# Products k'v by head in half-column tiles, one state update per pair of batches, and new hand-written orders, in a gated linear attention kernel with a GELU MLP

## The chip, the cores and the metric

The kernel runs on one core of one Trainium2 chip. The core has a matrix engine (TensorE, PE in the profile, with PEld for its weight loads), a vector engine (VectorE, DVE), an activation engine (ScalarE, ACT), GpSimd (POOL) and a synchronising engine (SyncE, SP); the last two mostly issue transfers here. Each engine takes its instructions in the order in which the program gives them; semaphores make one engine wait for another. The metric is the time of one execution on the device in microseconds, lower is better.

## The reference

Per batch and head, a state of 48x48 decays row by row with a gate and takes up an outer product at each of 768 steps; the output of a step is the query times the state. The results of the 8 heads side by side (384 values a token) go through a two-layer MLP with the tanh form of GELU.

```python
batch, n_heads, seq, head_dim = (4, 8, 768, 48)
for t in range(S):
    state = alpha[:, :, t, :, None] * state + np.einsum('bhd,bhe->bhde', k[:, :, t], v[:, :, t])
    y[:, :, t] = np.einsum('bhd,bhde->bhe', q[:, :, t], state)
...
n_tokens, d_model, d_ff = (3072, 384, 2048)
h = x @ w_in
g = 0.5 * h * (1.0 + np.tanh(c * (h + 0.044715 * h * h * h)))
return (g @ w_out).astype(np.float32)
```

## The kernel before

**Tiling.** The 768 steps are cut into 6 chunks of 128. Batches go two at a time, so there are 12 "pairs" m = 0 to 11: pair m is chunk m // 2 of batches 0 and 1 (m even) or 2 and 3 (m odd). Inside a chunk the recurrence becomes products. With b the running product of the gates, q' = q b (`qp`) and k' = k / b (`kp`), the output is mask(q' k'^T) v plus q' times the state that the chunk starts with, and the next state is (k'^T v + state) times the last row of b.

**A pair, step by step**, by the names that its tasks carry: `ln` (ACT, logarithm of the gate), `cum` (PE, running sums by a triangular matrix), `b` and `binv` (ACT, exponentials), `qp` and `kp` (DVE), `t` and `ev` (transposes of q' and k' on PE and their copies out; in pairs 6 to 11 the transfer `turn` instead), `attn` (PE, line 552: k' times q' per head, and in pairs 2 to 11 also line 561: q' times the old state), `mask` (DVE, line 571), `y` (PE, lines 617 and 627), `x` (copy out), `tx` and `xe` (transposing x; a `turn` in pairs 6 to 11), `kv` (PE, line 581) and `st` (DVE, lines 606 and 608). Then the MLP of that pair: eight tasks `l1` (PE, line 658, six products of 256 columns each), eight `gelu` (ACT), `l2` (PE, line 677, four products of 384 columns a task, four tasks a batch), `ot` (copy out on ACT or DVE) and `store` (SP).

**Heads in 64 places.** q' and k' hold each head in 64 columns, 48 filled and 16 zero, so that two heads fill the 128 columns of the array, and after the transposes two heads lie on top of each other in rows 0 to 63 and 64 to 127. Lines 484, 552 and 561 use the array cut into two halves by rows, one head in each (in the profile 64\*128).

**kv and st before.** Line 581 takes a pair of heads at once: 128 weight columns (both k' heads) times 96 columns of v (both v heads). Of the four 48x48 blocks of the result two are of use, head with head; the other two, head with the other head, are carried along unused. A batch has four such products, and the state of a batch is a tile of 128 x (4 x 96). `carry` then adds the old state (line 606, DVE; not in chunk 0) and multiplies by the last row of b (line 608, DVE), one task for each batch. `attn` reads the useful block of the state: `st[sl, p, self.D * o:self.D * o + self.D]`. Pairs 0 and 1 are laid out differently ("packed"): their k' is turned back (line 516) before kv, batch by batch.

**What sets the order.** A planner class holds tasks with costs (`W`, `COST`), and `FIRST` gives a list of steps such as `P:kv2.0` (PE, task kv of pair 2, first one) that fixes the order of all tasks on all engines. The list is complete, so each engine's order is that list. `fill` steps are idle products on zeros in the early part of PE's order. The planner's costs decide nothing where the list is complete. A list `firsts` made every `l2` task depend on all first-layer tasks of pairs 0 and 1. PSUM is shared out in tagged buffers; kv, y and the transposes share the tag `yk` with two buffers.

Of the kernel before, what the change touches and what calls it, by code (L numbers as in the profile page):

```python
# [17 lines left out]
    qk2=910, qk1=500, ev8=650, ev4=350, mask=640, st=1090, st0=545, tr=270, attn2=590, inter2=220, vb=320, vb_act=480, ring=1300, ring_issue=670, out=2050, lead=600, receipt=1400, receipt_hw=1000, xc=520, xe=330, ot=540,  # L18
# [153 lines left out]
class _Kernel:  # L172
# [21 lines left out]
        P:tx1.1 V:xe1.1 A:gelu0.5 P:l10.6 P:l11.0 A:gelu0.6 P:l11.4 P:l11.3 P:l11.5 A:gelu1.0 A:gelu1.4 A:gelu1.3 P:l11.2 A:gelu1.5 A:gelu1.2 P:l11.7
        A:gelu1.7 P:l11.1 P:l11.6 A:gelu1.1 P:l20.0 A:ln2.0 P:l20.3 P:l20.7 P:cum2.0 P:kv1.0 P:l20.11 P:l20.4 A:b2.0 A:binv2.0 A:ln2.1 P:cum2.1 A:b2.1
        V:st1.0 V:kp2.0 V:qp2.0 P:kv1.1 V:st1.1 G:load.33 G:load.34 G:load.35 G:load.36 G:load.37 V:qp2.1 P:l20.1 G:load.38 P:l20.5 P:l20.8 A:binv2.1
        V:kp2.1 A:gelu1.6 V:tr2.0 V:tr2.1 P:t2.0 A:ev2.1 V:ev2.0 V:tr2.2 V:tr2.3 P:l20.12 G:load.39 G:load.40 G:load.41 G:gate.2 G:load.42 G:gate.3
        G:load.43 G:gate.4 G:load.44 A:ot0.0 P:l20.15 P:attn2.0 A:ot0.3 P:l20.2 V:mask2.2 V:mask2.3 P:l20.9 P:l20.6 A:ln3.0 P:cum3.0 A:b3.0 V:mask2.0
        V:mask2.1 P:y2.0 P:l20.13 V:x2.0 P:y2.1 A:x2.1 V:qp3.0 P:l20.10 P:tx2.0 A:binv3.0 P:tx2.1 A:ot0.1 V:xe2.0 V:xe2.1 P:l20.14 A:ot0.2 P:kv2.0
        V:kp3.0 P:l12.6 P:l12.0 A:gelu2.0 A:gelu2.6 P:l12.5 V:st2.0 P:t3.0 A:gelu2.5 P:l12.1 A:ev3.1 V:tr3.0 P:l12.3 V:tr3.1 V:ev3.0 P:kv3.0 P:l12.7  # L200
        P:kv2.1 A:gelu2.1 P:l12.4 A:gelu2.7 A:gelu2.3 A:gelu2.4 P:l12.2 V:tr3.2 P:l22.4 V:tr3.3 V:st3.0 V:st2.1 P:attn3.0 A:gelu2.2 P:l22.5 P:l22.6
        V:mask3.2 V:mask3.3 A:ln4.0 P:cum4.0 P:l22.0 A:ln5.0 V:mask3.0 V:mask3.1 A:b4.0 P:y3.0 P:l22.7 A:x3.0 P:y3.1 P:kv3.1 V:qp4.0 P:l22.1 A:binv4.0
        A:x3.1 P:l22.2 A:ot2.1 P:tx3.1 V:st3.1 S:store0.0 V:tr4.0 V:xe3.1 P:cum5.0 P:tx3.0 V:xe3.0 V:kp4.0 P:l22.3 P:l13.0 A:binv5.0 A:b5.0 A:ot2.0
        P:l13.3 S:store0.3 P:t4.0 V:tr4.1 V:tr4.2 V:tr4.3 S:store2.1 V:ev4.0 P:l13.4 P:l13.2 V:ev4.1 P:kv4.0 A:gelu3.0 A:gelu3.3 A:gelu3.2 A:gelu3.4
        P:l13.5 A:gelu3.5 G:gate.5 G:load.45 G:gate.6 G:load.46 G:gate.7 G:load.47 G:gate.8 G:load.48 G:gate.9 G:load.49 G:gate.10 G:load.50 G:gate.11
        G:load.51 G:gate.12 G:load.52 G:gate.13 G:load.53 G:gate.14 G:load.54 G:gate.15 G:load.55 G:gate.16 G:load.56 G:gate.17 G:load.57 G:gate.18
        P:kv4.1 P:l13.6 P:l13.1 A:gelu3.6 P:l13.7 V:st4.0 V:st4.1 P:attn4.0 A:gelu3.1 P:l23.0 P:l23.1 A:gelu3.7 S:store2.0 S:store0.1 V:qp5.0 V:tr5.0
        A:ln6.0 V:mask4.2 V:mask4.0 V:mask4.3 V:mask4.1 V:kp5.0 P:l23.2 P:y4.0 P:l23.3 V:ot3.0 S:store3.0 P:y4.1 A:x4.0 A:x4.1 P:cum6.0 P:l23.4 A:b6.0
        P:tx4.0 V:xe4.0 P:tx4.1 V:xe4.1 P:l23.5 A:binv6.0 V:qp6.0 P:t5.0 A:ev5.1 A:ln7.0 V:ev5.0 P:l23.6 P:l23.7 P:attn5.0 P:l14.0 A:ot3.1 V:tr6.0
        V:tr5.1 V:tr5.2 V:mask5.0 S:store0.2 P:l14.4 P:l14.3 V:mask5.1 A:gelu4.0 A:gelu4.4 S:turn6.0 P:l14.6 S:store3.1 A:gelu4.3 A:gelu4.6 V:mask5.2  # L210
        V:mask5.3 P:y5.0 A:x5.0 V:kp6.0 V:tr6.1 V:tr6.2 P:l14.5 V:tr5.3 P:l14.2 A:gelu4.5 A:gelu4.2 P:y5.1 P:l14.1 A:gelu4.1 P:l14.7 P:kv5.1 V:x5.1
        V:tr6.3 P:kv5.0 A:gelu4.7 P:l24.0 P:cum7.0 A:b7.0 A:binv7.0 V:st5.1 P:l24.4 V:st5.0 P:kv6.0 S:turn6.1 V:st6.0 V:qp7.0 P:l24.5 P:l24.1 P:l24.2
        A:ln8.0 P:tx5.0 P:tx5.1 P:cum8.0 V:xe5.1 V:xe5.0 V:kp7.0 A:binv8.0 P:l24.3 V:ot4.0 P:l24.6 A:b8.0 P:l24.7 A:ot4.1 P:attn6.0 V:mask6.0 P:l15.0
        V:mask6.1 P:l15.2 P:l15.4 P:l15.5 V:mask6.2 V:kp8.0 V:mask6.3 P:y6.0 A:gelu5.0 A:gelu5.2 A:gelu5.4 P:l15.6 P:l15.1 V:x6.0 A:gelu5.6 A:gelu5.5
        P:y6.1 V:qp8.0 A:x6.1 S:turn7.0 P:l15.3 P:kv6.1 P:l15.7 A:gelu5.1 P:l25.4 S:turn7.1 P:l25.0 A:gelu5.3 P:l25.5 P:l25.6 A:gelu5.7 A:ln9.0
        V:st6.1 P:attn7.0 P:l25.1 V:mask7.2 P:l25.7 V:mask7.3 G:load.58 G:gate.19 G:load.59 G:gate.20 G:load.60 S:turn6.2 P:l25.2 A:ot5.1 V:mask7.0
        P:cum9.0 A:binv9.0 G:gate.21 G:load.61 G:gate.22 V:mask7.1 V:tr8.0 P:l25.3 P:y7.0 P:y7.1 P:l16.0 V:ot5.0 V:tr7.0 V:tr7.1 A:gelu6.0 A:x7.0
        P:l16.5 P:l16.7 P:l16.3 V:x7.1 S:store4.0 S:turn8.0 P:kv8.1 P:kv8.0 A:gelu6.7 A:gelu6.5 A:gelu6.3 S:turn7.2 V:tr8.1 V:tr8.2 P:l16.6 A:gelu6.6
        P:l16.4 A:gelu6.4 P:l16.1 P:l16.2 A:gelu6.1 A:gelu6.2 V:tr8.3 V:st8.1 V:st8.0 V:tr7.2 V:tr7.3 P:kv7.1 V:st7.1 V:kp9.0 P:kv7.0 P:l26.0 P:l26.1
        P:l26.4 P:l26.5 P:l26.2 S:turn8.1 A:ln10.0 A:b9.0 V:tr9.0 V:tr9.1 V:tr9.2 V:tr9.3 G:load.62 G:gate.23 G:load.63 G:gate.24 G:load.64 G:gate.25  # L220
        V:qp9.0 P:cum10.0 A:binv10.0 P:l26.3 P:l17.0 P:l26.6 P:l26.7 A:ot6.0 A:b10.0 S:turn9.1 A:gelu7.0 P:l17.6 A:gelu7.6 V:ot6.1 V:st7.0 P:l17.1
        A:gelu7.1 P:l17.2 P:l17.3 A:gelu7.2 P:attn8.0 S:turn9.0 V:mask8.0 V:mask8.1 A:gelu7.3 P:l17.7 P:l17.4 A:gelu7.4 A:gelu7.7 P:l17.5 V:mask8.2
        A:gelu7.5 P:l27.0 G:load.65 P:y8.0 V:mask8.3 A:x8.0 P:l27.4 P:y8.1 P:l27.5 P:l27.6 P:l27.1 V:x8.1 V:qp10.0 P:kv9.0 V:kp10.0 A:ln11.0 P:cum11.0
        A:binv11.0 A:b11.0 P:l27.7 P:l27.2 S:turn8.2 P:l27.3 S:store4.1 V:st9.0 P:attn9.0 V:kp11.0 S:store5.1 V:qp11.0 A:ot7.0 A:ot7.1 S:turn10.1
        P:l18.0 S:turn10.0 A:gelu8.0 S:store6.1 P:l18.3 V:mask9.0 V:mask9.1 P:l18.1 A:gelu8.1 A:gelu8.3 P:l18.7 P:l18.5 V:mask9.2 S:turn11.1 V:mask9.3
# [479 lines left out]
    def tasks(self):  # L705
# [221 lines left out]
        n = 0  # L927
# [108 lines left out]
```

## Time and profile before

| | |
|---|---|
| median of 3 runs | 174.98 us (174.98, 182.13, 174.59) |
| the profiled execution, its own time | 173.77 us |
| its span, first to last instruction | 171.9 us |
| clock granted to TensorE | 1.000 |
| DMA traffic | 29.40 MB, mean 171 GB/s |
| transfers out to landing, stores of 192 KB | 3.0 us |

The profile is one execution. It gives the busy time of each engine, the busy share in 40 slices, the chain of work that ended last, the groups of instructions by source line with their mean durations and the idle time ahead of them, and the transfers. The time of a product in these views is its latency, not its share of the stream; what it costs the stream is read from the starts of neighbours.

### The profile page before, as it was taken

What the parts mean: (1) busy time and instruction counts of PE and PEld (TensorE: products, weight loads), DVE (VectorE), ACT (ScalarE), POOL (GpSimd) and SP (SyncE); (2) the same over time, 40 slices, a digit from 0 to 9 for tenths busy, and PEclk for the clock granted to TensorE, in tenths of its full rate; (3) what the DMA queues carried; (4) which work ended last, traced back from release to release, by engine and by line L of the source; (5) the groups of instructions that cost most, each with busy time, mean ns of one, the idle gap of its engine ahead of it and who ended that gap; (6) DMA issues with size and microseconds to landing.
All of it is one profiled execution on the core that took longest, in us unless ns stands there. A gap on an engine that the chain in (4) does not pass through costs nothing.

```text
span 171.9 us, 4595 instructions
## 1 busy us (share of the span) xinstructions
PE 166.3 (97%) x1909; PEld 129.8 (75%) x1909; DVE 107.7 (63%) x210; ACT 125.5 (73%) x205; POOL 63.0 (37%) x88
## 2 busy tenths in 40 slices
PE   7999999999999999999999999999999999999991
PEld 2566899666886896797697797796797978987860
DVE  6499820588978999998892898865947550100100
ACT  4578889897999798899779499868882636651412
POOL 2396546986504674933565435320000000000000
PEclk9999999999999999999999999999999999999999
DMA  4999999999999999999999999897967504001212
GB/s 138 311 268 217 199 247 230 231 230 228 256 208 96 257 218 241 169 165 242 145 224 213 158 226 138 181 233 60 232 186 148 147 1 114 4 0 40 101 48 92
DMA packets 51541, 29.40 MB, mean 171 GB/s; under 512 B 39616, under 2 KB 47936, under 8 KB 51520
## 3 DMA queue, kind: packets, MB, share of 16 engines
q0 software_dynamic: 26464, 17.70, 62.3%
q1 hardware_dynamic: 24512, 11.01, 30.8%
q10 hardware_dynamic: 544, 0.39, 0.8%
q8 instruction: 15, 0.25, 0.6%
q14 instruction: 6, 0.05, 0.1%
HBM read 25.17 MB, written 4.72 MB: 174 GB/s over the span
## 4 chain that ended last, share of the span: by engine, by line
PE 91%; DMA 3%; ACT 3%; DVE 0%; issue 0%; DVEq 0%
PE hT L658 37%; PE acc L677 37%; PE at L552 4%; DMA k<-in_k_dram 3%; PE yps L627 2%; PE cum L416 2%; PE kv L581 2%; PE qkT_ps L484 1%; PE xT_ps L646 1%; PE qkT_ps L470 1%; PE yps L561 1%; ACT qkT L508 1%; PE k_ps L516 1%; ACT L318 1%; PE idle L327 1%; PE yps L617 1%
## 5 line engine op out<-in xcount | busy, mean ns | idle before, releaser
L658 PE MATMUL hT<-xT,w_in 128*128 128x256 bf16 x576 | 69.4, 273 | 0.0
L677 PE MATMUL acc<-w_out,gT 128*128 128x384 bf16 (+3 forms) x416 | 68.9, 314 | 0.0
L664 ACT ACTIVATE gT<-hT 128x512 bf16<-128x512 f32 x96 | 53.6, 600 | 15.2 <-PE hT L658 13.1
L658 PEld LDWEIGHTS <-w_in 128*128 128x128 bf16 x576 | 60.6, 114 | 1.2 <-DMA w_in<-in_moe_w_in_dram 0.3
L677 PEld LDWEIGHTS <-gT 128*128 128x128 bf16 x416 | 37.4, 98 | 20.2
L571 DVE TENSOR_TENSOR atm<-at,ut 128x512 bf16<-128x512 f32 x48 | 30.1, 683 | 8.2 <-PE at L552 8.0
L689 DVE COPY ot<-acc 128x384 f32<-128x384 f32 (+2 forms) x9 | 4.3, 488 | 20.0 <-PE acc L677 20.0
L689 ACT COPY ot<-acc 128x384 f32<-128x384 f32 (+1 forms) x17 | 7.9, 472 | 11.6 <-PE acc L677 9.3
L595 DVE STREAM_TRANSPOSE tr<-b 32x256 f32<-32x256 f32 x32 | 14.0, 438 | 1.4 <-ACT b L449 0.8
L346 POOL DMA_DIRECT2D k<-in_k_dram x11 | 12.2, 1111 | 5.7 <-DMA v<-in_v_dram 1.7
L346 POOL DMA_DIRECT2D a<-in_alpha_dram x11 | 12.3, 1117 | 4.4 <-issue 1.7
L460 DVE TENSOR_TENSOR qp<-q,b 128x768 bf16<-128x768 f32 (+1 forms) x15 | 11.9, 792 | 2.8 <-ACT b L449 2.6
L346 POOL DMA_DIRECT2D vb<-in_v_dram x11 | 12.2, 1105 | 3.6 <-issue 1.9
L346 POOL DMA_DIRECT2D q<-in_q_dram x11 | 12.2, 1112 | 2.5 <-DMA w_out<-in_moe_w_out_dram 1.0
L449 ACT ACTIVATE binv<-cum 128x768 bf16<-128x768 f32 (+1 forms) x15 | 10.1, 684 | 3.3 <-PE cum L416 3.3
L460 DVE TENSOR_TENSOR kp<-k,binv 128x768 bf16<-128x768 f32 (+1 forms) x15 | 11.9, 791 | 0.5 <-ACT binv L449 0.5
L318 ACT ACT_TABLE_LOAD x9 | 11.5, 1283 | 0.9 <-PEq L1020 0.7
L449 ACT ACTIVATE b<-cum 128x768 f32<-128x768 f32 (+1 forms) x15 | 10.3, 685 | 2.0 <-PE cum L416 1.5
L664 ACT ACT_TABLE_LOAD x9 | 11.5, 1283 | 0.2
L606 DVE TENSOR_TENSOR stmp<-kv,st 128x384 f32<-128x384 f32 x16 | 8.9, 555 | 1.9 <-PE kv L581 1.2
L608 DVE TENSOR_TENSOR st<-stmp,tr 128x384 bf16<-128x384 f32 x16 | 8.9, 558 | 0.6
L399 ACT ACTIVATE la<-a 128x768 f16<-128x768 f32 (+1 forms) x11 | 8.5, 784 | 0.1
(74 smaller groups left out, 144.8 us busy)
## 6 DMA issues: line engine op xcount, KB each, us to landing
out_dram<-ot SPq DMA_DIRECT2D x19, 192.0 KB, 3.0
a<-in_alpha_dram POOLq DMA_DIRECT2D x9, 384.0 KB, 7.8
q<-in_q_dram POOLq DMA_DIRECT2D x9, 384.0 KB, 8.8
k<-in_k_dram POOLq DMA_DIRECT2D x9, 384.0 KB, 6.9
vb<-in_v_dram POOLq DMA_DIRECT2D x9, 192.0 KB, 6.3
w_in<-in_moe_w_in_dram POOLq DMA_DIRECT2D x4, 384.0 KB, 8.9
w_out<-in_moe_w_out_dram POOLq DMA_DIRECT2D x4, 384.0 KB, 11.0
out_dram<-ot SPq DMA_DIRECT2D x9, 96.0 KB, 1.9
```

The costliest lines, as they stand in the source:

```text
L318: nc.scalar.add_instruction(mybir.InstLoadActFuncSet(name=nc.get_next_instruction_name(), act_func_set_id=i, engine=mybir.EngineType.Activ ...
L346: dma(u[t][:, lo:hi].rearrange("t b h d -> t (b h) d"), src.rearrange("b h s d -> s (b h) d")[c * C:(c + 1) * C])
L449: self.nc.scalar.activation(u[n].rearrange("t i h d -> t i (h d)")[:, lo:hi], cum, AF.Exp, scale=1.0 if n == "b" else -1.0)
L460: self.nc.vector.tensor_tensor(out, rows, b, op=ALU.mult)
L571: self.nc.vector.tensor_tensor(u["atm", i][:, o], u["at", i][o], self.ut[:, None, :].to_broadcast([self.C, self.H // 2, self.C]), op=ALU.mult)
L595: self.nc.vector.transpose(u["tr"][f:f + 32, :, 0:32], rows[:, lo:lo + H * 2 * D].rearrange("t (g n) -> t g n", n=2 * D)[:, :, 0:32])
L606: nc.vector.tensor_tensor(s, acc, old, op=ALU.add)
L608: nc.vector.tensor_tensor(new, acc, end[:, :, None].to_broadcast([C, H // 2, 2 * D]), op=ALU.mult)
L658: self.nc.tensor.matmul(h[:, s].rearrange("p (g t) -> p g t", t=self.C), w_in[:, j, nt % 4 + s], self.xT[c % self.NX][:, lo:hi, j], start= ...
L664: return lambda e: self.nc.scalar.activation(self.gT[c % self.NG][:, nt:nt + 2, lo * self.C:hi * self.C], f.pop(("h", c, lo, nt)), AF.Gelu ...
L677: self.nc.tensor.matmul(f["acc", c, b][:, lo:hi], self.gT[c % self.NG][:, nt, b * self.C:(b + 1) * self.C], self.w_out[:, nt, lo:hi], star ...
L689: self.copy(e)(f["ot", c, b][:, sl], f["acc", c, b] if half is None else f["acc", c, b, half][:, sl])
```

## The change

Three things change. The product k'v is made head by head: 64 weight columns (one head of k') times 48 columns (the same head of v), the first head of a pair of heads into the left 64 columns of the array and partitions 0 to 63 of PSUM, the second into the right 64 columns and partitions 64 to 127. A batch has eight such products where it had four. The state holds these diagonal blocks alone, 48 columns a pair of heads, and one tile holds both batches of a pair; outside the packed pairs 0 and 1, `kv` is one task for both batches and `st` one update for both, which waits for both batches' products, old states and readers. The list of steps is new, and `firsts` is gone. In the packed pairs kv and st stay one task a batch.

```diff
-    qk2=910, qk1=500, ev8=650, ev4=350, mask=640, st=1090, st0=545, ...
+    qk2=910, qk1=500, ev8=650, ev4=350, mask=640, st=1090, st0=380, ...
...
-        self.state = [[const.tile([C, H // 2, 2 * D], BF16, name=f"st{b}_{i}") for i in range(2)]
-                      for b in range(B)]
+        self.state = [[const.tile([C, 2, H // 2, D], BF16, name=f"st{g}_{i}") for i in range(2)] for g in range(B // 2)]
...
-                    st = self.state[b + i][c % 2]
+                    st = self.state[b // 2][c % 2][:, i]
...
-                            nc.tensor.matmul(y[o][:, i, p, :], u["T"][sl, 0, i, p, :], st[sl, p, self.D * o:self.D * o + self.D],
+                            nc.tensor.matmul(y[o][:, i, p, :], u["T"][sl, 0, i, p, :], st[sl, p, :],
...
-            kv = u["kv", i] = self.tile("yk", [C, H // 2, 2 * D], F32, "kv")
-            for p in range(H // 2):
-                nc.tensor.matmul(kv[:, p, :], u["kn" if u["packed"] else "kp"][:, i, 2 * p:2 * p + 2, :].rearrange("t h d -> t (h d)"),
-                                 u["vb"][:, i, 2 * p:2 * p + 2, :].rearrange("t h d -> t (h d)"),
-                                 start=True, stop=True)
+            kv = u["kv", units[0]] = self.tile("yk", [C, len(units), H // 2, D], F32, "kv")
+            for n, i in enumerate(units):
+                for p in range(H // 2):
+                    for o in range(2):
+                        nc.tensor.matmul(kv[64 * o:64 * o + 64, n, p, :], u["kn" if u["packed"] else "kp"][:, i, 2 * p + o, :],
+                                         u["vb"][:, i, 2 * p + o, :], start=True, stop=True, skip_group_check=True)
...
-                s = self.sb.tile([C, H // 2, 2 * D], F32, tag="stmp", bufs=1, name="stmp")
-                nc.vector.tensor_tensor(s, acc, old, op=ALU.add)
+                s = self.sb.tile([C, 2, H // 2, D], F32, tag="stmp", bufs=1, name="stmp")[:, lo:hi]
+                nc.vector.tensor_tensor(s, acc, self.state[g][c % 2][:, lo:hi], op=ALU.add)
                 acc = s
-            nc.vector.tensor_tensor(new, acc, end[:, :, None].to_broadcast([C, H // 2, 2 * D]), op=ALU.mult)
+            nc.vector.tensor_tensor(new.rearrange("f u p d -> f (u p) d"), acc.rearrange("f u p d -> f (u p) d"),
+                                    end[:, :, None].to_broadcast([C, (hi - lo) * H // 2, D]), op=ALU.mult)
...
+            for units in ((0,), (1,)) if u["packed"] else ((0, 1),) if c < NCH - 1 else ():
...
+                kv = s.add("kv", {"PE": W["kv"] * len(units)}, P + 30 + j, self.kv(u, units), ks + [vin[x] for x in units])
+                st = s.add("st", {"DVE": W["st"] if c else W["st0"]}, P + 30 + j, self.carry(u, units, c, i),
+                           [kv] + be + ([states[2 * i, c - 1], states[2 * i + 1, c - 1], ys[2 * i, c - 1], ys[2 * i + 1, c - 1]] if c else []))
...
-                if m < 2:
-                    firsts.append(t)
...
-                          gs[m if m else b // 2][2 * part:2 * part + 2] + [loads["w", "out", min(part, 3)]] + firsts, stream=n - 16)
+                          gs[m if m else b // 2][2 * part:2 * part + 2] + [loads["w", "out", min(part, 3)]], stream=n - 16)
```

The list of steps is the same up to `V:xe0.1` (the work of pair 0 and the beginning of pair 1) and different from there to its end; it is too long to be shown. Its last tasks are now layer 2 of pair 9, where they were layer 2 of pair 10.

More of the change, by code (lines that the diff above doesn't have):

```diff
@@ L17 @@
     cum=330, cum_packed=1500, t16=560, t4=225, attn=340, kv=170, inter=170, intra=205, tx=168, l1_4=655, l1_2=340, l2=655,
-    qk2=910, qk1=500, ev8=650, ev4=350, mask=640, st=1090, st0=545, tr=270, attn2=590, inter2=220, vb=320, vb_act=480, ring=1300, ring_issue=670, out=2050, lead=600, receipt=1400, receipt_hw=1000, xc=520, xe=330, ot=540,
+    qk2=910, qk1=500, ev8=650, ev4=350, mask=640, st=1090, st0=380, tr=270, attn2=590, inter2=220, vb=320, vb_act=480, ring=1300, ring_issue=670, out=2050, lead=600, receipt=1400, receipt_hw=1000, xc=520, xe=330, ot=540,
     ev8_act=960, ev4_act=520, xc_act=450, xe_act=450, ot_act=450,
@@ L194 @@
[L194 to L225, printed above, removed]
@@ L234 @@
-        S:store11.2 P:l110.6 V:ot9.0 S:store9.0 P:l110.1 A:gelu10.6 V:ot11.3 S:store11.3 S:store11.0 A:gelu10.1 P:l110.7 P:l110.5 S:store9.1
-        A:gelu10.7 P:l210.4 P:l210.5 P:l210.0 P:l210.1 A:gelu10.5 P:l210.6 P:l210.2 P:l210.7 A:ot10.1 P:l210.3 A:ot10.0 S:store10.1 S:store10.0
+        P:attn1.0 V:xe0.1 G:load.23 G:load.24 G:load.25 G:load.26 G:load.27 G:load.28 G:load.29 G:load.30 G:load.31 G:load.32 G:load.33 G:load.34
+        G:load.35 G:load.36 P:t1.2 P:l10.0 V:kp1.1 V:mask1.0 G:load.37 G:load.38 V:mask1.1 A:ev1.2 P:t1.3 A:vb1.0 A:ev1.3 P:t1.4 P:l10.1 P:attn1.1
@@ new lines @@
+        P:l10.3 P:l10.2 P:y1.0 V:ev1.4 A:gelu0.0 A:gelu0.1 P:l10.5 V:mask1.2 A:gelu0.3 V:mask1.3 V:vb1.1 P:y1.1 V:x1.0 P:tx1.0 V:xe1.0 A:x1.1 P:l10.4
+        P:tx1.1 P:l10.7 A:gelu0.2 A:gelu0.5 A:gelu0.4 V:xe1.1 P:l11.0 A:gelu0.7 P:t1.5 P:l11.3 A:gelu1.0 A:gelu1.3 P:l11.7 P:l10.6 A:gelu1.7 A:gelu0.6
+        P:l11.1 A:gelu1.1 P:l11.4 A:gelu1.4 P:l11.5 P:l11.2 P:l20.0 P:l20.4 P:l11.6 A:gelu1.5 P:l20.3 A:gelu1.2 G:load.39 G:load.40 A:ln2.0 P:cum2.0
+        A:binv2.0 A:b2.0 V:ev1.5 P:kv1.1 P:kv1.0 P:l20.7 V:st1.0 P:l20.8 V:qp2.0 V:st1.1 V:kp2.0 A:ln2.1 P:cum2.1 A:binv2.1 V:kp2.1 G:load.41 G:gate.2
@@ new lines @@
+        G:load.42 G:gate.3 P:l20.1 P:l20.5 A:b2.1 A:gelu1.6 V:qp2.1 P:l20.11 P:t2.0 V:ev2.1 P:l20.12 A:ot0.0 P:l20.15 V:ev2.0 A:ot0.3 P:attn2.0
+        V:tr2.0 V:tr2.1 P:l20.9 A:ln3.0 P:l20.13 P:l20.2 P:l20.6 V:mask2.0 G:load.43 V:mask2.1 V:mask2.2 P:y2.0 V:mask2.3 P:y2.1 A:ot0.1 V:tr2.2
+        P:cum3.0 P:l20.10 V:tr2.3 A:x2.0 A:x2.1 P:tx2.0 V:xe2.0 P:tx2.1 P:l20.14 A:b3.0 V:xe2.1 S:store0.0 A:binv3.0 A:ot0.2 P:kv2.0 V:qp3.0 P:l12.0
+        P:l12.4 P:l12.7 P:l12.6 V:st2.0 V:kp3.0 P:t3.0 A:gelu2.0 V:tr3.0 V:tr3.1 V:ev3.0 A:gelu2.4 A:gelu2.7 A:ev3.1 A:gelu2.6 P:l12.3 A:gelu2.3
@@ new lines @@
+        P:attn4.0 A:gelu3.1 A:gelu3.3 V:mask4.0 G:gate.4 G:load.44 S:store0.3 G:gate.5 G:load.45 G:gate.6 G:load.46 G:gate.7 G:load.47 S:store0.1
+        G:gate.8 G:load.48 G:gate.9 G:load.49 G:gate.10 G:load.50 G:gate.11 G:load.51 P:l13.6 S:store2.0 S:store0.2 P:l23.0 P:l23.4 V:mask4.2
+        A:gelu3.6 V:mask4.1 V:mask4.3 P:y4.0 P:l23.1 P:y4.1 V:x4.0 V:tr5.0 V:qp5.0 A:ln6.0 P:l23.5 P:cum6.0 A:x4.1 P:tx4.1 P:tx4.0 V:xe4.0 V:xe4.1
+        A:binv6.0 V:kp6.0 S:turn6.1 P:l23.6 P:l23.2 A:b6.0 P:t5.0 P:l23.3 A:ev5.1 V:ev5.0 V:tr5.1 P:l23.7 P:attn5.0 V:mask5.0 A:ot3.0 A:ot3.1 P:l14.0
@@ new lines @@
+        P:l14.2 A:ln7.0 P:l14.5 V:mask5.1 A:gelu4.0 A:gelu4.2 A:gelu4.5 P:l14.1 P:l14.6 A:gelu4.6 A:gelu4.1 G:gate.12 G:load.52 G:gate.13 G:load.53
+        P:l14.3 A:gelu4.3 V:mask5.2 P:y5.0 V:mask5.3 V:tr5.2 V:tr5.3 P:l14.4 A:gelu4.4 P:l14.7 V:qp6.0 G:gate.14 G:load.54 G:gate.15 G:load.55
+        G:gate.16 G:load.56 G:gate.17 G:load.57 G:gate.18 A:gelu4.7 V:x5.0 P:y5.1 V:x5.1 V:tr6.0 V:tr6.1 V:tr6.2 S:store3.0 P:l24.0 P:l24.1 P:cum7.0
+        S:store3.1 P:l24.2 P:tx5.0 V:xe5.0 A:b7.0 V:qp7.0 A:binv7.0 P:tx5.1 P:l24.3 S:turn6.0 P:kv5.0 P:l24.4 V:xe5.1 V:tr6.3 V:ot4.0 V:st5.0 V:kp7.0
@@ new lines @@
+        A:ln8.0 P:cum8.0 A:b8.0 A:binv8.0 P:l24.5 P:l24.6 P:l24.7 P:attn6.0 V:mask6.0 V:mask6.1 A:ot4.1 P:l15.0 A:gelu5.0 P:l15.4 P:l15.6 A:gelu5.6
+        V:mask6.2 V:mask6.3 A:gelu5.4 P:l15.2 P:y6.0 S:turn7.0 P:y6.1 S:turn7.1 P:l15.1 P:l15.7 A:gelu5.2 V:x6.0 G:load.58 G:gate.19 G:load.59
+        G:gate.20 G:load.60 G:gate.21 G:load.61 G:gate.22 V:x6.1 S:turn6.2 P:l15.5 P:l15.3 G:load.62 G:gate.23 S:store4.1 P:kv6.0 A:gelu5.7 A:gelu5.1
+        A:gelu5.3 S:store4.0 V:tr7.0 V:tr7.1 V:qp8.0 V:st6.0 P:l25.4 G:load.63 G:gate.24 A:gelu5.5 P:l25.5 P:l25.6 P:attn7.0 P:l25.0 V:kp8.0 P:l25.7
@@ new lines @@
+        G:load.64 G:gate.25 P:l25.1 V:mask7.0 V:ot5.1 V:tr7.2 V:mask7.2 P:l25.2 P:l25.3 P:l16.0 S:turn8.0 V:mask7.3 P:l16.4 A:ln9.0 V:mask7.1 P:y7.1
+        P:y7.0 P:l16.5 V:ot5.0 V:x7.0 A:gelu6.0 A:gelu6.4 P:l16.2 A:gelu6.2 A:gelu6.5 V:x7.1 P:l16.1 P:l16.6 A:gelu6.6 P:kv7.0 P:l16.7 A:gelu6.1
+        P:l16.3 P:cum9.0 P:kv8.0 P:l26.4 V:tr7.3 S:turn7.2 A:gelu6.7 A:gelu6.3 S:turn8.1 P:l26.0 P:l26.1 P:l26.5 P:l26.6 P:l26.7 A:binv9.0 A:ln10.0
+        A:b9.0 P:cum10.0 P:l26.2 P:l26.3 P:l17.0 V:st7.0 V:tr8.0 V:tr8.1 V:tr8.2 V:tr8.3 V:st8.0 V:kp9.0 V:qp9.0 V:tr9.0 V:ot6.1 S:turn9.0 V:tr9.1
@@ new lines @@
+        A:binv10.0 A:b10.0 P:l17.3 P:l17.7 A:gelu7.0 P:kv9.0 A:gelu7.3 S:turn9.1 V:tr9.2 V:tr9.3 V:ot6.0 P:l17.6 V:kp10.0 A:gelu7.7 P:l17.1 A:gelu7.6
+        P:l17.2 A:gelu7.1 V:st9.0 P:attn8.0 V:mask8.0 V:mask8.2 P:l17.5 A:gelu7.2 P:l17.4 V:mask8.1 V:mask8.3 P:l27.4 P:y8.0 P:l27.5 A:gelu7.4 P:y8.1
+        A:gelu7.5 P:l27.6 V:x8.0 V:x8.1 S:turn8.2 P:l27.7 V:ot7.1 P:l27.0 A:ln11.0 P:cum11.0 A:b11.0 A:binv11.0 P:l27.1 P:l27.2 P:l27.3 P:attn9.0
+        P:l18.0 V:qp10.0 V:qp11.0 S:store5.1 A:ot7.0 V:mask9.0 V:mask9.1 S:store6.0 S:store6.3 S:store5.0 P:l18.4 S:turn10.1 G:load.65 P:l18.3
@@ L596, in last_row, with carry @@
         return emit
-    def carry(self, u, i, c, b):
+    def carry(self, u, units, c, g):
         nc, H, C, D = self.nc, self.H, self.C, self.D
         def emit(e):
-            acc, old, new = u["kv", i], self.state[b][c % 2], self.state[b][(c + 1) % 2]
-            end = u["tr"][:, 4 * i:4 * i + 4, 31] if u["sums"] == "DVE" else u["bend"][:, i]
+            lo, hi = units[0], units[-1] + 1
+            acc, new = u["kv", lo], self.state[g][(c + 1) % 2][:, lo:hi]
+            end = u["tr"][:, 4 * lo:4 * hi, 31] if u["sums"] == "DVE" else u["bend"][:, lo:hi].rearrange("f u p -> f (u p)")
             if c > 0:
-                s = self.sb.tile([C, H // 2, 2 * D], F32, tag="stmp", bufs=1, name="stmp")
-                nc.vector.tensor_tensor(s, acc, old, op=ALU.add)
+                s = self.sb.tile([C, 2, H // 2, D], F32, tag="stmp", bufs=1, name="stmp")[:, lo:hi]
+                nc.vector.tensor_tensor(s, acc, self.state[g][c % 2][:, lo:hi], op=ALU.add)
                 acc = s
-            nc.vector.tensor_tensor(new, acc, end[:, :, None].to_broadcast([C, H // 2, 2 * D]), op=ALU.mult)
+            nc.vector.tensor_tensor(new.rearrange("f u p d -> f (u p) d"), acc.rearrange("f u p d -> f (u p) d"),
+                                    end[:, :, None].to_broadcast([C, (hi - lo) * H // 2, D]), op=ALU.mult)
         return emit
@@ L891, in tasks @@
             xcs[0].take("x", *txs)
-            for j in range(2):
-                b, k, turned = 2 * i + j, kp[j], turns[j]
-                if c < NCH - 1:
-                    if u["packed"]:
-                        tb = s.add("t", {"PE": W["t4"]}, P + 29 + j, self.turn_back(u, j), turned)
-                        k = s.add("ev", {"DVE": W["ev4"], "ACT": W["ev4_act"]}, P + 29 + j, self.turned_back(u, j), [tb])
-                        tb.take("yk", k)
-                        users.append(tb)
-                        backs.append(tb)
-                    kv = s.add("kv", {"PE": W["kv"]}, P + 30 + j, self.kv(u, j), [k, vin[j]])
-                    st = states[b, c] = s.add("st", {"DVE": W["st"] if c else W["st0"]}, P + 30 + j, self.carry(u, j, c, b),
-                                              [kv] + be + ([states[b, c - 1], ys[b, c - 1]] if c else []))
-                    kv.take("yk", st)
-                    vs.append(kv)
-                    kvs.append(kv)
-                    cs.append(st)
+            for units in ((0,), (1,)) if u["packed"] else ((0, 1),) if c < NCH - 1 else ():
+                j, ks = units[0], [kp[x] for x in units]
+                if u["packed"]:
+                    tb = s.add("t", {"PE": W["t4"]}, P + 29 + j, self.turn_back(u, j), turns[j])
+                    ks = [s.add("ev", {"DVE": W["ev4"], "ACT": W["ev4_act"]}, P + 29 + j, self.turned_back(u, j), [tb])]
+                    tb.take("yk", ks[0])
+                    users.append(tb)
+                    backs.append(tb)
+                kv = s.add("kv", {"PE": W["kv"] * len(units)}, P + 30 + j, self.kv(u, units), ks + [vin[x] for x in units])
+                st = s.add("st", {"DVE": W["st"] if c else W["st0"]}, P + 30 + j, self.carry(u, units, c, i),
+                           [kv] + be + ([states[2 * i, c - 1], states[2 * i + 1, c - 1], ys[2 * i, c - 1], ys[2 * i + 1, c - 1]] if c else []))
+                for x in units:
+                    states[2 * i + x, c] = st
+                kv.take("yk", st)
+                vs.append(kv)
+                kvs.append(kv)
+                cs.append(st)
             if u["packed"]:
```

30 lines of the change are left out of this document (17 added, 13 removed).

## The prediction

> **What bounds the kernel now.** I read the page from the top: the busy times, then the forty slices.
>
> ```profile
> span 171.9 us, 4595 instructions
> ...
> PE 166.3 (97%) x1909; PEld 129.8 (75%) x1909; DVE 107.7 (63%) x210; ACT 125.5 (73%) x205; POOL 63.0 (37%) x88
> ...
> PE   7999999999999999999999999999999999999991
> ```
>
> TensorE (PE) is busy in every slice but the first and the last. A busy PE may still be one that waits inside a pipelined product, so I went on to the sums by window, the waits of PE and the end of the chain in order of time.
>
> ```profile
> core 0: us, PE busy (x) PEld busy (x) DVE busy (x) ACT busy (x) POOL busy (x), PEclk, DMA share, GB/s
> 16.00:168.40 152.40, 152.27 (x1773) 121.73 (x1772) 96.07 (x173) 114.69 (x182) 53.22 (x68) 1.00 0.96 165
> 0.00:16.00 16.00, 14.01 (x137) 8.03 (x138) 11.63 (x38) 10.37 (x24) 9.83 (x20) 1.00 0.91 237
> ```
> ```profile
> PE idle L327 <- DVE ones L990: 1.2, 1, 1.2
> PE qkT_ps L470 <- DVE kp L460: 0.3, 1, 0.3
> PE k_ps L516 <- ACT qkT L508: 0.2, 1, 0.2
> ```
> ```profile
> 55.20 1.30 PE acc L677 x8
> ...
> 160.50 2.62 PE hT L658 x24
> 163.12 5.21 PE acc L677 x32
> 168.36 0.48 ACT ot L689
> ```
>
> From 16.0 to 168.4 us PE idles 152.40 - 152.27 = 0.13 us at full clock, and the waits put down to it are 1.7 us, the largest of them at the very start. The products of the dense layers run at one steady pace, near the start as at the end: 1.30 / 8 = 0.1625 us for 384 columns of layer 2, 2.62 / 24 = 0.109 us for 256 columns of layer 1. So PE's own instruction stream is the time. The 16 us ahead of it are set by the first loads and by ACT and DVE turn by turn, and behind it come one copy and one store, 171.9 - 168.4 = 3.5 us. Outside the span lie 173.77 - 171.9 = 1.87 us. Anything that does not shorten PE's stream, the first 16 us or the tail is worth nothing here.
>
> **The change, part by part.** First the products k'v, line 581.
>
> ```profile
> L581 PE MATMUL kv<-vb,kp x64: 203/206/206, 43.4 to 134.1; 128*128 128x96 bf16 x64
> L581 PE MATMUL kv<-vb,kn x16: 202/204/206, 12.6 to 33.4; 128*128 128x96 bf16 x16
> ```
> ```profile
> 43.55 0.17 PE kv L581 x4
> ...
> 78.47 0.34 PE kv L581 x8
> ```
>
> Removed: one batch's four products (two heads at once, 128x96) take 0.17 us of the stream, a pair of batches 0.34 us, whether they stand apart or together. Of the 20 units, two lie ahead of 16 us and 18 behind: 18 x 0.17 = 3.06 us.
>
> Added: 16 products a pair, each with 64 weight columns and 48 moving ones, by turns in the left and the right 64 columns of the array. That half-column shape occurs nowhere in the trace of before. What does occur is the array cut in half by rows (64*128), and it shows that cutting costs something by itself:
>
> ```profile
> 33.23 0.33 PE L581 MATMUL kv<-vb,kn 128*128 128x96 bf16 x4
> 33.39 2.11 PE L677 MATMUL acc<-w_out,gT 128*128 128x384 bf16 x12
> 35.44 0.41 PE L484 MATMUL qkT_ps<-ident,qp 64*128 64x64 bf16 x16
> 35.68 0.40 PE L484 MATMUL qkT_ps<-ident,kp 64*128 64x64 bf16 x16
> 36.01 1.47 PE L677 MATMUL acc<-w_out,gT 128*128 128x384 bf16 x8
> 37.42 0.78 PE L552 MATMUL at<-qkT 64*128 64x128 bf16 x16
> ```
>
> The first column is the start. Twelve layer-2 products from 33.39 would hand over at 33.39 + 12 x 0.1625 = 35.34; the first half-row product starts at 35.44: 0.10 us to go in. Sixteen half-row transposes take 35.68 - 35.44 = 0.24 us, 15 ns each, so 32 would end at 35.92, and the next whole-array product starts at 36.01: 0.09 us to come out. Eight more from 36.01 would hand over at 37.31 and the next half-row product starts at 37.42, so about 0.01 us more is lost on the way. One trip into a cut array and back costs 0.20 us. A load of weights goes with every product here as there.
>
> The Trainium skill, page "TensorEngine Tiling (Array Packing)", section "Key Properties", says that changing the tiling mode, not merely the tile, drains TensorE. For cuts by rows this trace agrees, at the 0.20 us just worked out; no run here shows it yet for cuts by columns.
>
> The order of the built programs says how often the trip is made: 36 changes of cut before (18 trips, all for half rows), 58 after (29 trips), because none of the new products stands next to a half-row group. So there are 11 new trips: kv of pair 0's two batches (two trips of 8 products), of pair 1 (its two batches stand next to each other, one trip of 16) and of the eight pairs 2 to 9 (16 each). All other PE work is the same in number and shape, the 17 filler products included.
>
> What the 16 products cost inside a trip is the unknown, and these rows bound it:
>
> ```profile
> 51.20 0.20 PE yps L561 x16
> ...
> 53.97 0.20 PE yps L627 x8
> ...
> 56.50 0.17 PE xT_ps L646 x3
> ```
>
> Low end 0.20 / 16 = 13 ns: half-row products of 48 columns, the two halves running beside each other. Middle 0.20 / 8 = 25 ns: 48 columns on the whole array, one after another, each with its own weights. High end 0.17 / 3 = 57 ns: the slowest small product, 128 columns with weights of its own. Below the low end I see nothing, since two halves are two halves. I take 15 ns, the half-row transposes above: a product in each half by turns, narrow, with a fresh load each, is the nearest row in kind. Then a trip of 16 is 0.20 + 16 x 0.015 = 0.44 us against 0.34 us removed, +0.10 us; nine such trips after 16 us make **+0.9 us**. At 13 ns it is 9 x 0.07 = +0.6, at 25 ns 9 x 0.26 = +2.3, at 57 ns 9 x 0.77 = +6.9 us.
>
> The two trips of pair 0 lie ahead of the dense part:
>
> ```profile
> 15.49 0.33 PE L581 MATMUL kv<-vb,kn 128*128 128x96 bf16 x4
> 15.96 0.33 PE L646 MATMUL xT_ps<-ident,x 128*128 128x128 bf16 x3
> ```
>
> Each grows by 0.20 + 8 x 0.015 - 0.17 = 0.15 us. The second ends at 15.66 and PE then stands until 15.96, a cover of 0.30 us; the first stands in the part where PE idles 16.00 - 14.01 = 1.99 us. I cost both at nothing, 0.3 us without the cover.
>
> **The state update** (lines 606, 608) works on 48 columns a head pair rather than 96, for both batches in one instruction.
>
> ```profile
> L606 DVE TENSOR_TENSOR stmp<-kv,st 128x384 f32<-128x384 f32 x16 | 8.9, 555 | 1.9 <-PE kv L581 1.2
> L608 DVE TENSOR_TENSOR st<-stmp,tr 128x384 bf16<-128x384 f32 x16 | 8.9, 558 | 0.6
> L608 DVE TENSOR_TENSOR st<-kv,bend 128x384 bf16<-128x384 f32 x4 | 2.2, 558 | 7.9 <-PE kv L581 7.9
> ```
>
> The 16 pairs of instructions become 8 of the same size, so 8 x (0.555 + 0.558) = 8.9 us leave DVE. That is idle time gained on an engine with 63% load, for which PE waited 1.5 us in all by the waits above; worth 0 us. The first update of pair 1 (two batches still apart) and of pair 0 halve in width; at most 4 x 0.28 = 1.1 us of DVE in the start, where st is not what the chain waits for: 0. One new wait comes with it: the update of batch 0 now waits for batch 1's products too. Its reader is the group of line 552 two pairs on: pair 2's products stand at 43.55, and pair 4's group at
>
> ```profile
> 64.08 0.55 PE at L552 x16
> ```
>
> so some 20 us cover it; masks and scalings queued behind the update in DVE wait a fraction of a microsecond: 0. The carried products (line 561) read the state contiguously with the same 48 columns: 0.
>
> **The orders.** POOL issues in the same order as before; SP has the same transfers, its stores and transposing transfers interleaved anew; ACT keeps its 18 table loads and hands eight copies to DVE, at most 8 x 0.557 = 4.5 us of the time that DVE gained:
>
> ```profile
> L637 DVE CAST x<-yps 128x384 bf16<-128x384 f32 x9 | 4.9, 557 | 5.8 <-PE yps L627 5.7
> ```
>
> With only 0.13 us idle to win, a new order can only add. Its tightest place is the first use of the weights:
>
> ```profile
> 20.69 0.85 PE hT L658 x6
> ```
> ```profile
> L658 PEld LDWEIGHTS <-w_in 128*128 128x128 bf16 x576 | 60.6, 114 | 1.2 <-DMA w_in<-in_moe_w_in_dram 0.3
> ```
>
> These six products (0.655 us at the pace) waited 0.2 us for the third part of w_in, and the new order asks for it by one task of 0.65 us sooner or later: 0 to +0.2 us. The removed rule that layer 2 waits for all first-layer products lets its first one start one task earlier, in place of another: 0. The tail still ends in one full copy and one store of 192 KB: 0.
>
> **Sum:** -3.06 + 9 x 0.44 = +0.9 us. The profiled run would go from 173.77 to about 174.7; that run was 1.2 us quicker than the median of the runs, 174.98, so the same sum on the median gives **175.9 us**.
>
> **The rivals.** *No overlap of halves*: column halves share the rows' data path and run one after another at 25 ns. For it: each product needs all 128 rows, as line 627's do. Time 174.98 + 2.3 + 0.2 of the start = 177.5 us.
>
> *Weight loads become the bound*, the case on the slower side: 64 columns are loaded in a slower way than 128 and show at every product in every one of the nine trips. For it: every load in this trace is 128 columns wide, so nothing shows how a narrow one goes. Against it: half-row loads stayed hidden at 15 ns. At the 57 ns bound it is 174.98 + 6.9 = 181.9 us; past (3.5 / 9 + 0.34 - 0.20) / 16 = 33 ns a product it is over 2% slower. The Trainium skill speaks for this case: the tiling page, section "Restrictions", says column tiling switches fast weight load off, and the page "TensorE: Matmul & The Clock Gate", section "LDWEIGHTS (loading the stationary operand)", gives columns / 1.2 ns. By it a 64-column load is an estimated 53 ns, and the sum would be +6.4 us if no two loads overlap, +2.6 us if the halves load beside each other.
>
> *No pause for column cuts*: if only row cuts drain the array, a trip costs 16 x 0.015 = 0.24 against 0.34 us, and 9 x 0.10 = 0.9 us are won: 174.1 us; at 13 ns and with the 0.13 us of idle time gone, 173.6 us. Against it: all cuts in the trace pay.
>
> **How the numbers follow.** Forecast 0.45, no overlap 0.24, weight loads 0.18, no pause 0.13. Range 173.6 to 180.0 us: from the best of the last rival, over the forecast with its early +0.5, the no-overlap case and pairs up to 42 ns a product; most of the weight-load case stays out, some 0.12, and 0.06 below. Two per cent is 3.5 us, about what a measurement of this kernel can tell from no change. Faster by more than that has no case above, 0.03; slower takes the weight-load case and the dense end of no overlap, 0.21; within 2%: 0.76.
>
> **What would show it.** Right: in the timeline around line 582, whole-array product to whole-array product in 0.44 us for 16 kv products, 0.10 us of it ahead of them; 58 changes of cut; DVE 4 to 9 us less busy; PE busy to the tail with the stream about 1 us longer. Pace 25 ns or 50 ns there, or no gap ahead of the first, picks the rival. Wrong altogether: a stretch of idle PE after 16 us, a later start of the dense part, or a longer tail.

## The result, and the profile after

| | before | changed |
|---|---|---|
| median of 16 runs each, taken together | 173.96 us | 175.55 us |
| ratio to before, 95% interval | | 1.0073 (1.0049 to 1.0097) |
| the profiled execution, its own time | 173.77 us | 175.65 us |
| its span | 171.9 us | 173.9 us |

The change makes the kernel slower by 0.73%, 0.0073 x 173.96 = 1.3 us (0.9 to 1.7), inside the 2%. The median of before is lower here than in the three runs shown ahead of the prediction. Some executions of both kernels take longer than the others, up to 182.13 us before and 180.34 us changed; the medians count them, the ratios, here and below, leave them out.

The page of the changed kernel, the lines that answer to those of before:

```profile
span 173.9 us, 4734 instructions
...
PE 167.4 (96%) x1989; PEld 129.8 (75%) x1989; DVE 103.6 (60%) x202; ACT 121.8 (70%) x197; POOL 63.9 (37%) x88
...
PE   7999999999999999999999999999899999999991
```

PE has 80 products more and is 1.1 us busier; DVE is 4.1 us less busy, which bought nothing. One slice, the 30th, has come down from 9 to 8. The sums by window show idle time that was not there before (0.98 us from 16 to 170 us, against 0.13), and the waits of PE put 0.8 us of it down to one place, layer 1 waiting for the copy `ot`:

```profile
16.00:170.00 154.00, 153.02 (x1853) 121.38 (x1852) 92.54 (x166) 111.17 (x174) 54.04 (x68) 1.00 0.97 164
```
```profile
PE idle L326 <- DVE ones L991: 1.2, 1, 1.2
PE hT L660 <- ACT ot L691: 0.8, 1, 0.8
PE k_ps L515 <- ACT qkT L507: 0.2, 1, 0.2
PE qkT_ps L469 <- DVE xT L652: 0.2, 1, 0.2
```

The timeline of PE around one joint kv task, first column the start:

```profile
42.91 0.81 PE L679 MATMUL acc<-w_out,gT 128*128 128x384 bf16 x4
43.65 0.43 PE L582 MATMUL kv<-vb,kp 128*64 128x48 bf16 x16
44.02 1.17 PE L660 MATMUL hT<-xT,w_in 128*128 128x256 bf16 x9
```

Four layer-2 products from 42.91 hand over at 42.91 + 4 x 0.1625 = 43.56. The first half-column product starts at 43.65, 0.09 us later, and the next whole-array product at 44.02: 0.46 us for the trip, where the whole-array products of before took 0.34 us. Nine such trips are 9 x 0.12 = 1.1 us.

The chain of waits of the changed kernel no longer runs through PE alone. Around the wait for `ot` it reads, first column the start, second the duration:

```profile
119.24 0.21 PE yps L629 x8
...
119.47 0.57 DVE x L639
...
120.06 1.21 SPq L533
...
121.32 4.03 DMA out_dram<-ot
...
125.43 0.49 ACT ot L691
...
125.96 1.14 PE hT L660 x9
```

From below: layer 1 waits for a PSUM buffer that holds a finished result; ACT copies that result out at 125.43, late, because all five output tiles are taken; the tile that it waits for is released by a store that SP issued at 121.32, behind a transposing transfer that itself waited for `x`. The products of layer 1 show the hole:

```profile
124.35 0.85 PE L660 MATMUL hT<-xT,w_in 128*128 128x256 bf16 x6
...
125.96 1.58 PE L660 MATMUL hT<-xT,w_in 128*128 128x256 bf16 x13 [0.77 <-ACT ot L691]
```

The last of the six starts at 124.92 us and would be followed at 125.03; the next one starts at 125.96. PE lost 0.93 us there, from start to start of its products.

### The profile page after: what moved, and what is told of

It reads as the page before. It is cut to its first block, busy times and chain, and to the rows that moved or that the text cites. A ratio compares the mean times of both kernels' runs of the same rounds, so it can differ in the third digit from the quotient of the medians.

```text
span 173.9 us, 4734 instructions
## 1 busy us (share of the span) xinstructions
PE 167.4 (96%) x1989; PEld 129.8 (75%) x1989; DVE 103.6 (60%) x202; ACT 121.8 (70%) x197; POOL 63.9 (37%) x88
## 4 chain that ended last, share of the span: by engine, by line
PE 73%; DMA 17%; POOL 4%; SPq 2%; issue 1%; ACT 1%; DVE 0%; ACTq 0%; POOLq 0%
PE acc L679 31%; PE hT L660 31%; DMA w_out<-in_moe_w_out_dram 12%; DMA k<-in_k_dram 3%; PE at L551 3%; DMA out_dram<-ot 2%; PE yps L629 2%; POOL w_in L358 2%; PE kv L582 2%; PE cum L415 1%; SPq L342 1%; PE yps L560 1%; PE qkT_ps L483 1%; PE xT_ps L648 1%; SPq L533 1%
## 5 line engine op out<-in xcount | busy, mean ns | idle before, releaser
L691 DVE COPY ot<-acc 128x384 f32<-128x384 f32 (+3 forms) x14 | 6.9, 495 | 19.8 <-PE acc L679 19.7
L691 ACT COPY ot<-acc 128x384 f32<-128x384 f32 x12 | 5.8, 483 | 14.2 <-PE acc L679 12.1
L639 DVE CAST x<-yps 128x384 bf16<-128x384 f32 x12 | 6.4, 555 | 12.1 <-ACT gT L666 6.4
L551 PEld LDWEIGHTS <-qkT 64*128 64x128 bf16 x192 | 5.4, 94 | 3.8 <-issue 1.9
```

The lines of the kernel that those rows point to most:

```text
L551: nc.tensor.matmul(at[o][:, p, :], t[sl, 1, p, :], t[sl, 0, p, :], start=True, stop=True)
L691: self.copy(e)(f["ot", c, b][:, sl], f["acc", c, b] if half is None else f["acc", c, b, half][:, sl])
```

## The experiments

All times are compared with the kernel of before on the same chip in the same session.

**The change without its new orders.** The new kv, state and update, with the list of steps of before; joint tasks stand where the later of the two batch tasks stood:

```diff
-        ... P:kv2.0 P:l12.6 P:l12.0 ... P:kv3.0 P:l12.7 P:kv2.1 ... V:st3.0 V:st2.1 ...
+        ... P:l12.6 P:l12.0 ... P:l12.7 P:kv2.0 ... V:st2.0 ...
```

> The change without its new orders: half-column products and the joint update, in the order of before (for pairs 2 to 9 the joint kv stands where the later of the two batch tasks stood, the joint update likewise). Theory (the trips into the cut array are the cost): nine trips of 16 products at 0.45 us against 0.34 us are +1.0 us, plus up to 0.3 us at the start, so 0.5 to 0.8% slower than before. Rival (the new orders are the cost, half-column products are free): within 0.2% of before.

Measured: 1.0074 (1.0043 to 1.0105). The products and the joint update, without the new orders, carry a slowdown as large as the whole change's. Pair 1's two batches stand apart in this order, so it has ten trips after 16 us.

**The new orders with products of before.** The joint tile of 48 columns a head pair is kept; the four products of a batch are again 128x96 on the whole array, and overlap in what they write:

```diff
-                    for o in range(2):
-                        nc.tensor.matmul(kv[64 * o:64 * o + 64, n, p, :], u["kn" if u["packed"] else "kp"][:, i, 2 * p + o, :],
-                                         u["vb"][:, i, 2 * p + o, :], start=True, stop=True, skip_group_check=True)
+                    at = min((n * H // 2 + p) * D, end)
+                    nc.tensor.matmul(flat[:, at:at + 2 * D], u["kn" if u["packed"] else "kp"][:, i, 2 * p:2 * p + 2, :].rearrange("t h d -> t (h d)"),
+                                     u["vb"][:, i, 2 * p:2 * p + 2, :].rearrange("t h d -> t (h d)"), start=True, stop=True, skip_group_check=True)
```

> The new orders with the products of before in number and shape: per batch four whole-array products of 128x96, written with overlap into the joint tile of 48 columns a head pair, so that the state is left wrong; update and orders as changed. No cut by columns is left (36 changes of cut). Theory (trips): 1.0 to 1.3 us faster than the changed kernel, so 0 to 0.2% slower than before. Rival (the new orders are the cost): as slow as the changed kernel, 0.7% slower than before.

Measured: 0.9984 (0.9948 to 1.0020), level with before and 0.9% below the changed kernel, 1.6 us where 1.0 to 1.3 were expected, a difference that the intervals allow. The cost goes when the cut by columns goes, with orders and updates as changed. The rival that blames the orders falls twice.

**Six output tiles.**

```diff
-    BUFS = dict(ca=1, yk=2, ff=4, la=3, qp=4, kp=4, b=2, binv=2, kn=2, qkT=4, atm=6, x=2, ot=5, bend=2,
+    BUFS = dict(ca=1, yk=2, ff=4, la=3, qp=4, kp=4, b=2, binv=2, kn=2, qkT=4, atm=6, x=2, ot=6, bend=2,
```

> The changed kernel with six output tiles instead of five. In its profile one copy of a result on ACT waited at 125.4 us for a store to release its tile, and PE waited 0.93 us behind it. Theory (that wait belongs to the new order and costs its length): the wait is gone and the time falls by 0.5 to 0.9 us, to 0.2 to 0.4% slower than before. Rival (the wait is one of that execution, or another takes its place): time as the changed kernel, 0.7% slower than before.

Measured: 1.0039 (0.9999 to 1.0080). In its profile the wait for `ot` is gone and none has taken its place:

```profile
PE idle L326 <- DVE ones L991: 1.2, 1, 1.2
PE qkT_ps L469 <- DVE xT L652: 0.3, 1, 0.3
PE k_ps L515 <- ACT qkT L507: 0.2, 1, 0.2
PE yps L619 <- DVE vb L426: 0.2, 1, 0.2
```

The ratio is 0.0034 below the changed kernel's, 0.6 us, but the intervals overlap, so both kernels ran once more side by side.

> The changed kernel as it is, beside the next one on the same chip, to see whether PE's wait near 126 us comes back. Theory (the wait belongs to the new order and to five output tiles): PE stands for 0.5 us or more between 122 and 127 us again, and the time is 0.6 to 0.9% above before. Rival (an accident of one execution): no wait there, 0.4% above before.

> The changed kernel with six output tiles, beside the one above. Theory: no wait of PE near 126 us, 0.3 to 0.5% above before, so 0.2 to 0.5% below the one above. Rival: the two agree within 0.1%.

Measured: five tiles 1.0058 (1.0031 to 1.0086), six 1.0026 (0.9993 to 1.0060); medians 175.49 and 174.83 us. Five tiles fall just short of the 0.6 to 0.9% expected. The direction came twice, at 0.6 to 0.7 us; the intervals overlap again. None of the six profiles with six tiles and the new orders (this one, the one above and the four of the experiments below that use both) has a wait of PE between 118 and 131 us. The profile taken now with five tiles has two, between 123.7 and 128.5 us by the starts, and they are other waits:

```profile
PE at L551 <- DMA qkT<-kp: 2.0, 1, 2.0
PE hT L660 <- DMA xT<-x: 1.9, 1, 1.9
```

PE waits there for transposing transfers, which go out on SP's queue among the stores, and not for an output tile. The execution took 180.39 us, 5 us over the median, and the kernel of before has such long ones as well (181.46 us in the same session). So this profile does not show that the wait for a tile comes back; what held these two transfers stays open.

**Both edits together.** Whole-array products with overlap and six tiles:

> Both of the last two edits: whole-array products written with overlap (the state is left wrong) and six output tiles, in the new orders. If the costs of trips and of the store's wait add up: 1.5 to 2.2 us faster than the changed kernel, 0.1 to 0.5% faster than before. If either is absorbed by another wait: equal to before or slower.

Measured: 0.9986 (0.9938 to 1.0034), no different from whole-array products alone. The gains did not add up. Its profile names a new wait of the faster stream, 94.7 us into the span:

```profile
PE at L551 <- DMA qkT<-kp: 1.2, 1, 1.2
```

**The kernel of before with six output tiles.** The same edit in the kernel of before.

> The kernel of before with six output tiles instead of five. Theory (the wait for a store belongs to the new orders): no change, within 0.2% of before. Rival (output tiles are short in both): 0.2 to 0.5% faster than before, which would make it the best of all.

Measured: 1.0013 (0.9975 to 1.0050). No gain shows, and one of more than 0.25% lies outside the interval. So a shortage of output tiles shows in the new orders alone.

**Left half, then right half** (with six output tiles, as the next two).

```diff
-            for n, i in enumerate(units):
-                for p in range(H // 2):
-                    for o in range(2):
+            for o in range(2):
+                for n, i in enumerate(units):
+                    for p in range(H // 2):
```

> The changed kernel with six output tiles, and the products of a kv task in another order: all of the left half of the array first, then all of the right half. In the changed kernel's trace two neighbours in different halves start 3 ns apart and each pair of them takes 32 ns. Theory (the two halves work beside each other, and only because neighbours alternate): a product then takes some 30 ns, a trip of 16 grows from 0.36 to about 0.6 us in the chain, nine trips add 1.9 to 2.2 us, 1.4 to 1.7% slower than before. Rival (a product takes 16 ns by its issue, whatever half it is in): nothing changes, 0.4% slower than before.

Measured: 1.0120 (1.0086 to 1.0154). The timeline around the same task:

```profile
42.90 0.81 PE L679 MATMUL acc<-w_out,gT 128*128 128x384 bf16 x4
43.65 0.58 PE L582 MATMUL kv<-vb,kp 128*64 128x48 bf16 x16
44.16 1.07 PE L660 MATMUL hT<-xT,w_in 128*128 128x256 bf16 x8
```

From the first product to the next whole-array one it is 0.51 us against 0.37. With 0.10 us of it for coming out, a product takes (0.51 - 0.10) / 16 = 26 ns one half after the other, and (0.37 - 0.10) / 16 = 17 ns by turns. But the 26 ns are a mean over two paces. The starts of the sixteen single products in the trace lie 52, 32, 31, 32, 6, 26, 26, 5, 27, 5, 27, 31, 32, 32 and 31 ns apart, and nearly the same in all eight joint tasks. They fall into two series of eight, each with a first step of 52 ns and then steps of 31 or 32 ns; the second series begins when the first has three products still to start. The records do not name the half; I read the two series as the left and the right one. So a product takes 32 ns where its half works alone, and by turns two products take 32 ns: the halves work beside each other, and alternating neighbours gain 16 ns a product, a little more than the 14 expected. The time, 1.2% where 1.4 to 1.7% were expected, falls short because PE begins the right half's products before the left half's have all started, so that the middle of the task overlaps even in this order.

**A second trip.** One whole-array product between the two batches:

```diff
             for n, i in enumerate(units):
+                if n:
+                    nc.tensor.matmul(kv[:, n, 0, :], u["kp"][:, i, 0:2, :].rearrange("t h d -> t (h d)"), u["vb"][:, i, 0, :],
+                                     start=True, stop=True, skip_group_check=True)
                 for p in range(H // 2):
```

> The changed kernel with six output tiles, and one whole-array product of 48 columns between the two batches of each joint kv task; the next product overwrites what it writes. So each of the eight joint tasks makes two trips into the cut array instead of one. Theory (a trip costs 0.20 us whatever is in it): 8 x (0.20 + 0.025) = +1.8 us, 1.4% slower than before. Rival (the pause belongs to the work that stands around kv, not to the change of cut): below +0.5 us, at most 0.7% slower than before.

Measured: 1.0118 (1.0087 to 1.0149) where 1.4% was expected, 0.8 to 0.9% above the two measurements with six tiles and one trip.

```profile
42.77 0.81 PE L682 MATMUL acc<-w_out,gT 128*128 128x384 bf16 x4
43.51 0.31 PE L585 MATMUL kv<-vb,kp 128*64 128x48 bf16 x8
43.75 0.20 PE L581 MATMUL kv<-vb,kp 128*128 128x48 bf16 x1
43.88 0.31 PE L585 MATMUL kv<-vb,kp 128*64 128x48 bf16 x8
44.12 1.06 PE L663 MATMUL hT<-xT,w_in 128*128 128x256 bf16 x8
```

From the end of layer 2 (42.77 + 0.65 = 43.42) to the start of layer 1 it is 0.70 us where one trip took 0.46: 0.24 us for leaving, one product of 25 ns and coming back. The pause belongs to the change of cut.

**Every product twice** in the same trip:

```diff
-                for p in range(H // 2):
+                for p in range(H):
+                    p = p // 2
```

> The changed kernel with six output tiles, and every product of kv made twice in the same trip (the second writes the same values again). Theory (0.20 us a trip plus 16 ns a product): a trip of 16 grows to 32 products, from 0.36 to 0.62 us in the chain; nine of them and the two early ones add 2.3 to 2.6 us. Rival (narrow weight loads pile up in a longer run): above 25 ns a product, +3.6 us or more.

Measured in one execution: span 175.6 us against 172.6 with single products, +3.0 us. The timeline:

```profile
44.34 0.69 PE L583 MATMUL kv<-vb,kp 128*64 128x48 bf16 x32
44.96 0.74 PE L661 MATMUL hT<-xT,w_in 128*128 128x256 bf16 x5
```

44.96 - 44.34 = 0.62 us, as the theory said: 16 more products cost 0.25 us, 16 ns each. Nine trips make 2.3 us of the 3.0. The rest is lost before the first of the nine, which starts at 32.34 us against 31.59 with single products; that part of the span differs from profile to profile.

No version beat both kernels. The two with whole-array products in the new orders leave the state wrong and gain 0.16% at most, inside their intervals.

## Why the prediction was right

It said 175.9 us, +0.9 us on before, within 2%; measured were 175.55 us and +1.3 us (0.9 to 1.7). The starting point counted in the absolute number: it stood on a median of three runs 1 us above that of sixteen, while the difference came out 0.4 us too small, so that the absolute forecast is closer than its parts by luck.

*PE's stream is the time.* Right. DVE lost 4.1 us of work, 8.9 us in the first experiment (98.8 us against 107.7), and nothing came of it; PE's products in the cut array account for the slowdown, in the old order (first experiment) and by their removal (second).

*The trip.* Right in its parts. Forecast were 0.10 us in, 15 ns a product, 0.10 us out, 0.44 us; the trace has 0.09 us, 16 to 17 ns, 0.10 us and 0.46 us. The half-row transposes were a good row to price half-column products by. Nine trips are 1.1 us where 0.9 were forecast.

*Eleven trips, two at no cost.* The count held. The cover at the start can't be told: the first layer-1 product starts at these times in the changed kernel, in the old order with the new products, and with six output tiles:

```profile
17.12 0.49 PE L660 MATMUL hT<-xT,w_in 128*128 128x256 bf16 x3
```
```profile
16.22 0.82 PE L661 MATMUL hT<-xT,w_in 128*128 128x256 bf16 x6
```
```profile
16.96 0.71 PE L660 MATMUL hT<-xT,w_in 128*128 128x256 bf16 x5
```

Before it is 16.79 us. These starts scatter by 0.9 us from profile to profile, more than the 0.3 us in question.

*The orders can only add, and hardly do.* Wrong in both directions, and the errors cancel in part. The step that failed is "with only 0.13 us idle to win". A product that waits for its operand while the one ahead of it is still in the pipeline counts as busy time. In the trace of before, starts show what the sums by window hide:

```profile
51.99 0.81 PE L677 MATMUL acc<-w_out,gT 128*128 128x384 bf16 x4
52.84 0.32 PE L416 MATMUL cum<-la,ut_h 128*128 128x384 f16 x1
...
107.03 0.81 PE L677 MATMUL acc<-w_out,gT 128*128 128x384 bf16 x4
107.79 0.48 PE L416 MATMUL cum<-la,ut_h 128*128 128x384 f16 x2
```

The first cum should start at 51.99 + 0.65 = 52.64 and starts at 52.84, 0.20 us late; the last of seven such places loses 107.79 - 107.68 = 0.11 us; together, counting those of more than 0.05 us, they are 0.83 us. One of them, 0.19 us at 20.4 us, is the wait for w_in that the prediction names. It changes with the execution and not with the order alone: it is 0.53 us in the old order with the new products, nothing in the profile of the changed kernel, and 0.35 us at the same place in the second profile with six tiles. That leaves 0.64 us to the order. In the first profile with the new orders and six output tiles 0.14 us of such waits are left in two places. So the orders won about 0.5 us and, with five output tiles, gave some 0.6 to 0.7 us back near 126 us. I had checked weights, the tail and the state for new waits, not the output tiles and SP's queue, where the new order moves stores and transposing transfers past each other. The balance, 1.1 for trips, -0.5 for small waits, +0.7 at 126 us, is +1.3 us and lies inside the measured 0.9 to 1.7. That last term rests on two comparisons with overlapping intervals and on the profiles; that the orders alone win 0.5 us is read from single profiles and was not resolved by timing (0.9986 with whole-array products and six tiles, interval to both sides of 1).

*No overlap of halves* falls: where one half works alone the products start 32 ns apart, by turns 16. *Narrow weight loads become the bound* falls in size: 33 ns a product were needed for 2%. A half alone is slower, though, than the whole array with 48 columns (32 ns against 25), and the record of a load, which gives its latency, is longer for 64 columns than for 128, 112 ns in the changed kernel against 98 ns before:

```profile
L581 PEld LDWEIGHTS <-kp 128*128 128x128 bf16 x64 | 4.0, 98 | 0.5
```
```profile
L582 PEld LDWEIGHTS <-kp 128*64 128x64 bf16 x128 | 2.6, 112 | 1.9 <-issue 1.9
```

The Trainium skill ("TensorEngine Tiling (Array Packing)", section "Restrictions") excludes fast weight load from column tiling; that fits the 16 ns against the 13 ns of half-row products, which load 128 columns each, but no run separates loads from issue. By the Trainium skill, page "TensorE: Matmul & The Clock Gate", section "LDWEIGHTS (loading the stationary operand)", a 64-column load takes an estimated 53 ns; in one half alone a product with its load follows the last every 32 ns, so the measurement decides against that figure as a pace here. *No pause for column cuts* falls by the second trip: 0.24 us for each.

## What to carry to other kernels

Cutting the array saves only if the products saved outweigh the way in and out: here 16 half-column products cost 0.27 us against 0.34 us for 8 whole ones, and the 0.2 us around them turned a gain into a loss. Before relieving an engine, see whether the bounding engine waits for it; 9 us off DVE's updates were worth nothing. Where the bounding engine is pipelined, look for small waits in the starts of its instructions, not in its busy share, and follow a new order through every queue that it reorders, stores included.

## What the runs showed of the hardware that was not expected

Two half-column products in different halves start 3 ns apart and such a pair takes 32 ns; in the same half products start 32 ns apart. So alternating halves doubles the pace. With the left half's eight products ahead of the right half's in the program, the right ones, by the starts, began when three of the left were still to come, so that the whole task took 0.15 us longer than by turns and not the 8 x 32 = 256 ns of one half strictly after the other. By these starts PE does not keep to the program's order between the halves. Changing the cut costs the same 0.2 us for columns as for rows.
